# An attention and feed-forward kernel on one core: v moved to partitions 32 to 95, row copies by SyncE, masks on GpSimd, and a new order of the work

## The chip, the cores and the metric

The kernel runs on one core of a Trainium2 chip. The metric is the device time of one execution in microseconds (us), lower is better. Times before the change come from three runs; one further execution was taken with the hardware profiler, and its span (first to last instruction) and its own time stand in the table below.

The engines, by the names that the profile uses: TensorE (PE, its weight loads PEld), VectorE (DVE), ScalarE (ACT), GpSimd (POOL) and SyncE (SP). GpSimd and SyncE also issue transfers, which 16 DMA engines carry out.

## The reference

Four batches, eight heads, 768 positions, 64 elements to a head, all given in float32. Two stages: an attention with a narrow band and one summary key for each block of 32 positions, and a feed-forward layer whose rows are the heads of one position side by side.

```python
block, window = 32, 16
k_sum = k.reshape(B, H, 24, 32, D).max(axis=3)
v_sum = v.reshape(B, H, 24, 32, D).mean(axis=3)
scores_l = where(|i - j| < 16, scale * q @ k.T, -1e9)      # the band
scores_s = scale * q @ k_sum.T + log(32)                   # 24 summary keys
a = softmax(concat(scores_l, scores_s))
attn = a @ concat(v, v_sum)                                # 768 x 64 for each head
x = attn, heads side by side                               # 3072 x 512
h = x @ w_in                                               # 512 -> 2048
out = (h * clip(h + 3, 0, 6) / 6) @ w_out                  # 2048 -> 512
```

## The kernel before, in words

**Tiles.** A query tile has 64 positions. A band of half-width 16 around it touches at most 96 keys, so each query tile multiplies with 96 band keys and 24 summary keys, 120 rows in all. Keys stand in `kaug` (12 tiles of 96 + 24 columns for each pair of heads), queries in `qaug` (`qT` is its view without the first 32 columns), probabilities in `at`, values in `vaug`, of which there are two: batch b uses `vaug[b % 2]`. In `vaug` the partition is the key of the tile: rows 0 to 63 are the 64 positions of the tile, rows 64 to 95 the first 32 positions of the next tile (the "halo"), rows 96 to 119 the 24 block sums. Since the window reaches 64t to 64t + 95, the queries of tile t are positions 64t + 16 to 64t + 79: q is shifted by 16. A row of `vaug` holds 66 elements (132 bytes): 64 of v, and ones (or 32 for the summary rows) that make the softmax's denominator.

**Attention of one batch.** The scores matmul gives 120 x 768 for a pair of heads and half the positions (L519); ScalarE takes the exponential (L527); VectorE multiplies with the 0/1 band mask (L531; batch 0's first half has the mask added in the matmul instead); the values matmul (L632) is 120 deep; VectorE divides by the denominator (L663, L667); TensorE transposes the result (L682) into `x`, feature by position. The block sums of v are a matmul with a 0/1 matrix (`ind`, L552 and L567), copied out and spread over the 12 tiles: by VectorE and ScalarE in batches 0 and 1, by SyncE's transfers (L575) in batches 2 and 3.

**How k and q come in.** Batch 0 is loaded in rows and transposed by TensorE (L448, L493), q in two halves. Batches 1 to 3 are loaded "raw": 32 rows by 96 chunks of 32 elements, four loads for k (L367) and eight for q (L375, two of 16 rows for each group because of the shift), and VectorE transposes 32 x 32 blocks (L588, L592). There is one raw buffer each for k and q, so a batch's loads wait for the transposes of the batch before. v comes in four loads a batch (L385), the halo of batches 1 to 3 in one more load from memory (L393) and a small SyncE copy (L395); batch 0's halo is copied by VectorE or ScalarE.

**The feed-forward layer.** A tile s is half a batch (384 positions). F steps: for each of 16 blocks of 128 hidden features four matmuls of 384 columns into a bank `h` (L700), a relu on ScalarE (L705), a product on VectorE (L707). G steps: for each of three groups of 128 positions 16 matmuls of 512 columns, in quarters of four (L720), then a copy out (L432, a helper's line) and a store by SyncE (L730, L732). The two weight matrices are loaded in four pieces each (L417, L423).

**What sets the order of the work.** Every step is recorded with its engine, a cost, what it reads and writes and the buffers that it takes. `ORDER` is a list of all steps written out in the program. `Plan.run` goes through it, gives each step its buffer and its estimated begin, and the instructions are recorded in that order. Each engine works through its own instructions strictly in order, so what stands behind a waiting instruction waits with it; this holds for GpSimd's and SyncE's issues too. A name in the list reads so: `K21.0` is load 1 of k of batch 2, `Q`, `V`, `H` likewise for q, v and halo, `I` and `O` are the pieces of w_in and w_out, `k`, `q`, `s`, `u`, `h`, `v` are key, query, scores, block-sum, halo and values steps, `w21` the raw transposes of batch 2 and pair 1, `F` and `G` the feed-forward steps; `:A`, `:D` (and in the new list `:P`) say that a step that may run on several engines runs on ScalarE, VectorE or GpSimd. In the first 22 us, matmuls on a constant tile fill TensorE's gaps (L803).

Of the kernel before, what the change touches and what calls it, by code (L numbers as in the profile page):

```python
# [9 lines left out]
F32 = mybir.dt.float32  # L10
# [5 lines left out]
D = 64  # L16
# [5 lines left out]
VW = 66  # L22
# [7 lines left out]
c.0 K00.0 c.7 K01.0 c.10 c.11 c.12 c.13 c.9 c.1 Q000.0 K02.0 Q010.0 c.2 c.3 k00.0 k01.0 q010.0 k01.1 k01.4 k00.1 q010.1:A  # L30
k00.4 c.4 k00.3:A k01.2 s010.0 q030.0 q000.0 q000.1:A s030.0 s010.1 s010.2 q020.0 q020.1:A k00.2 q030.1:D k01.3:D k03.0
k03.1 k02.0 k02.1 V00.0 V01.0 c.6 V02.0 V03.0 I0.0 I1.0 Q001.0 s000.0 u00.0 s000.1 u01.0 k03.3:A k03.2 k02.2 u00.1:D u00.2:D
k03.4 u01.1:D s000.2 u01.2:A u00.3:D k02.4 h21.0:D k02.3:D u02.0 s020.0 s030.1 s020.1 s020.2 u03.0 h30.0:D h00.0:D h10.0:D
h01.0:D v00.0 v02.0 u03.1:D u03.2:D v00.2 u01.3:D v00.3 u02.1:A s030.2 h20.0:A u02.2:A Q011.0 I2.0 I3.0 O0.0 O1.0 O2.0 O3.0
K10.0 K11.0 K13.0 K12.0 v01.0 v01.2 v02.1 v00.1 v02.4 v00.4 v00.5 v02.2 v02.3 v02.5 v00.6 v01.1 v01.3 v01.4 v01.5 h31.0:A
v00.7:A u03.3:A q001.0 q011.0 q001.1:A q021.0 q021.1:A u02.3:D q011.1:D v01.6 v02.6 q031.0 s021.0 v01.7:A h11.0:D v02.7:D
c.5 c.8 s021.1 F00.0 F00.1 F00.2 F00.10 F00.3 F01.0 F01.1 s001.0 s001.1 s021.2 q031.1:D F00.4 F01.2 s001.2 F00.11 F00.12
s011.0 F00.13 F00.14 Q121.0 Q101.0 Q110.0 Q100.0 Q120.0 Q131.0 Q130.0 Q111.0 s011.1 s011.2 s031.0 F00.5 F00.6 F00.7 F01.9
F00.8 F00.9 F02.6 s031.1 F01.3 F02.7 F01.10 F01.4 s031.2 F02.8 v04.0 v03.0 F01.6 F01.11 F01.5 v03.1 v03.2 F01.7 F01.8 v04.1
F02.3 F02.4 F02.5 F02.9 v03.3 v03.4:A F02.10 v04.2 F00.15 F02.0 v05.0 v04.3 F00.16 F02.1 F02.11 F00.17 F02.2 v05.1 v05.2  # L40
F03.3 F03.9 F03.0 v04.4:A F03.4 v05.3 F03.1 F03.10 v05.4:A G01.0 F03.5 F03.11 F03.2 F03.6 F10.0 F03.7 F12.0 F03.8 F10.1
F10.3 F12.1 F10.2 F12.2 F10.6 F10.4 F10.9 F10.5 F10.7 F10.8 F11.0 F10.10 F10.11 F11.6 F11.1 F11.9 F11.2 F11.7 F11.8 F11.10
F11.11 F12.6 F12.7 F12.8 F12.9 F12.10 F12.11 w12.0 G01.1 F13.0 F13.1 w13.0 F13.2 w11.0 w13.3 w10.0 w12.3 G01.2 G01.3 F12.3
F13.9 G01.4:A G02.0 G02.1 G02.2 G02.3 F11.3 F13.10 w11.2:A F12.4 F12.5 G02.4:A w12.2:A F13.3 F11.4 F13.4 w10.2:A w13.2:A
w12.4 w11.3 w11.4 w11.1 w11.5:D G00.0 G00.1 s110.0 s110.1 s110.3 w12.1 w13.1 w12.5:D w13.5:A G00.2 G00.3 s120.0 s120.1
s120.3 w13.4 w10.1 F13.5 w10.3 F11.5 w10.4 w10.5:D F13.11 V10.0 V13.0 V11.0 V23.0 V12.0 H1.0 K20.0 K22.0 V20.0 K21.0 Q231.0
K23.0 Q220.0 V22.0 V21.0 Q200.0 Q221.0 Q201.0 Q211.0 Q210.0 Q230.0 s130.0 G00.4:A F13.6 G12.0 s130.3 s130.1 F13.7 G00.5
G01.5 H1.1 G02.5 s120.2 s110.2 s130.2 s100.0 s100.1 F13.8 s100.2 s110.4 s100.3 G12.1 u1.0 u1.1:A u1.3:A u1.5:A G12.2 G12.3
G12.4:A u1.4:D u1.2:D v10.0 s120.4 v10.1 v10.5 v10.6 v10.2 s100.4 u1.7:A u1.6:A u1.9:A G11.0 G11.1 v12.0 v10.3 v10.4:A
u1.8:A v12.1 v12.2 s130.4 G11.2 v10.7 v12.3 v10.8:D G11.3 v12.4:A v13.0 F20.0 F20.3 G11.4:A F20.1 F20.4 v13.5 v13.1 v13.2  # L50
v13.6 F20.9 v13.3 v15.0 F20.10 F20.2 F20.5 F20.11 v15.1 v15.2 F20.6 F21.0 F20.7 F20.8 F21.1 V30.0 V31.0 V32.0 V33.0 F21.2
w21.0 F21.6 G10.0 F21.7 v13.4:A F21.8 F21.3 v15.3 v13.7 F21.9 F22.3 F21.4 F21.5 w20.0 F22.0 G10.1 F21.10 F22.4 v15.4:A
F21.11 F22.1 F22.5 F22.9 F23.0 F22.2 w20.3 F22.10 F22.11 F23.1 w21.2:A v13.8:A F23.2 w22.0 F22.6 u2.0 F22.7 F22.8 w21.3
G10.2 F30.0 F23.6 G10.3 w22.2:A F30.1 w20.4 F30.2 F30.3 F23.3 G10.4:A w22.3 w22.4 G22.0 G22.1 w20.1 u2.1:A w20.2:A F23.7
F23.4 w20.5:A F30.4 G12.5 u2.3 u2.5 G11.5 u2.4 u2.2 F23.5 F23.8 w22.1 s200.0 s200.1 s200.3 F30.5 w22.5:A F31.6 F23.9 G22.2
w23.1 F23.10 F31.7 s220.0 F23.11 F31.8 w21.4 w21.1 w21.5:D F30.9 G22.3 F31.0 F31.3 s220.3 s220.1 s210.0 G22.4:A H2.0 Q301.0
Q330.0 w23.0 K32.0 Q311.0 H3.0 F31.1 w23.5:A Q310.0 Q300.0 Q320.0 Q331.0 F31.2 F31.4 s200.4 F30.10 F30.11 F31.5 G20.0 G20.1
F30.6 F32.3 F33.0 Q321.0 K33.0 K31.0 K30.0 s210.1 s210.3 w23.3 F30.7 w23.4 s200.2 F30.8 w23.2:A F32.4 F33.1 u3.0 u3.1:D
s220.2 F33.2 s220.4 s210.2 G20.2 s230.0 s230.1 s230.3 s230.2 F32.5 G20.3 F31.9 F32.9 F31.10 F31.11 G20.4:A H2.1 G10.5 u3.3
u3.5 H3.1 G20.5 G22.5 v20.0 v20.1 v20.5 v20.2 v20.6 F33.9 G32.0 F32.10 F33.10 v22.0 F33.3 v20.3 F33.11 F32.0 G32.1 F33.4  # L60
v20.4:A v20.7 F32.1 v20.8:A v22.1 v22.2 F33.5 s230.4 F32.2 s210.4 v22.3 F32.11 v22.4:A F33.6 F32.6 F33.7 F32.7 v23.0 F33.8
v23.1 F32.8 F40.0 F40.1 F41.3 G32.2 F40.9 G32.3 F40.10 F41.4 v23.2 F40.2 F40.11 F41.5 v23.5 v23.6 F42.3 F41.9 F42.4 F42.5
F43.0 v25.0 F41.10 G32.4:A v23.3 F41.11 F42.0 F40.6 G30.0 G30.1 v23.4:A F43.1 F42.1 F40.7 v25.1 w30.1 F42.2 F43.2 F40.8
F41.0 F41.1 F41.2 v25.2 F40.3 F40.4 w30.5:A w33.1 w32.1 F42.6 G30.2 G30.3 F42.9 G30.4:A F42.7 v23.7 v23.8:A F42.10 G21.0
G21.1 G21.2 F40.5 w31.0 F42.8 F42.11 F43.3 F43.4 w30.0 w30.3 F43.6 w30.4 F43.5 w31.3 G21.3 F43.7 w32.5:D G21.4:A G21.5 v25.3
F41.6 G31.0 F43.9 G31.1 G31.2 w31.4 F43.8 v25.4:A F41.7 w30.2:A w33.0 F43.10 w31.2:A F41.8 w31.1 w31.5:D w32.0 F43.11 s300.0
F50.9 G31.3 F50.0 s300.1 s300.3 G31.4:A s310.0 s310.3 F50.1 s310.1 G31.5 u3.2 u3.4 G32.5 G30.5 w33.2:A w32.2:D w33.3 w32.3
w33.5:D F50.2 G40.0 F53.0 F53.1 F50.10 w32.4 w33.4 F50.11 G40.1 G40.2 G40.3 G40.4:A s320.0 s320.1 s320.3 F51.0 F53.3 G42.0
F53.4 s330.0 F51.1 s330.3 s330.1 s310.2 s310.4 F53.2 F53.5 s320.2 s300.2 s330.2 F51.2 G42.1 G42.2 F51.6 F51.7 F51.8 F52.3
v30.0 v30.5 v30.1 v30.6 v30.2 F52.0 F52.1 F52.4 F50.3 v32.0 v32.1 F52.2 F52.5 G42.3 G42.4:A F50.4 v30.3 F52.9 s330.4 G41.0  # L70
F51.3 G41.1 F52.10 v30.4:A v32.2 v32.3 v30.7 F51.4 F50.5 s320.4 F52.11 F51.9 v30.8:A F51.10 F51.5 v32.4:A F50.6 F50.7 F51.11
F50.8 s300.4 F52.6 G41.2 F52.7 F52.8 G41.3 F60.0 F60.1 G41.4:D F60.3 v33.0 F60.4 F60.2 F53.9 F53.10 F53.6 F53.7 F53.8 v33.1
F53.11 F60.5 v33.5 v33.6 G50.0 G50.1 v33.2 G41.5 F62.3 G50.2 F61.9 F61.10 G50.3 F62.4 G50.4:A G42.5 F61.11 v33.3 F62.9 v35.0
G51.0 F60.9 F60.10 v33.4:D F62.5 v35.1 v35.2 v35.3 F62.10 v35.4:A F60.11 v33.7 F60.6 G51.1 G51.2 F60.7 F60.8 F62.11 G51.3
G51.4:D v33.8:A F61.3 F61.0 F61.6 F61.4 F61.1 F61.7 F61.2 F61.5 F61.8 G52.0 F63.3 F70.0 G52.1 F72.6 G52.2 F63.4 F70.1 F70.2
F63.5 F73.0 F63.9 F72.7 F73.1 F63.10 F72.8 F73.2 F63.11 G52.3 G51.5 G50.5 G40.5 F63.0 F62.0 F62.6 F62.1 G52.4:D F62.7 F62.2
G62.0 F62.8 F63.6 F63.1 F63.7 F63.2 G62.1 G62.2 F70.9 F70.6 F63.8 G62.3 F70.10 F70.7 F70.11 G62.4:D F70.3 F71.3 F71.4 F70.8
F71.5 G61.0 G61.1 F72.9 F72.10 F70.4 F72.11 F71.6 F71.7 F70.5 F71.8 G61.2 F73.3 F73.4 F73.5 G61.3 F72.3 F71.0 F71.9 G61.4:D
F71.1 F72.4 F71.2 F72.5 F71.10 F71.11 G60.0 F72.0 F73.6 G60.1 G60.2 G72.0 F73.7 F72.1 F72.2 G62.5 G61.5 G52.5 F73.8 F73.9
F73.10 F73.11 G72.1 G71.0 G71.2 G60.3 G72.2 G71.4 G71.6 G70.0 G60.4:A G71.7:A G71.1 G70.1 G71.8 G60.5 G71.3 G71.5 G71.9  # L80
G70.2 G70.3 G70.4:A G71.10:A G71.11 G70.5 G72.3 G72.4:D G72.5
"""

BANKS = ("S", "h", "o")


SLOW = 8.5
TURN = 0.11
LATER = 19.0
KRAW = 2.0  # L90
LAT = {"PE": 0.16, "ACT": 0.08, "DVE": 0.07}


# [8 lines left out]
class Op:  # L102
    def __init__(self, eng, cost, fn, prio, lat, alloc):
        self.eng, self.cost, self.fn, self.prio, self.lat, self.alloc = eng, cost, fn, prio, lat, alloc
        self.deps, self.bufs, self.end, self.begin, self.dma = set(), [], None, None, 0.0
        self.alloc = [] if alloc is None else alloc if isinstance(alloc, list) else [alloc]


class Plan:
# [11 lines left out]
    def op(self, eng, cost, fn, r=(), w=(), prio=0.0, alloc=None, dma=0.0, lat=None, free=(), touch=(), after=0.0, form="full"):  # L121
# [21 lines left out]
        o.deps.discard(o)  # L143
        self.ops.append(o)
        return o

    def run(self):

        named = {o.key: o for o in self.ops}
# [5 lines left out]
        for token in ORDER.split():  # L155
# [16 lines left out]
            for a in o.alloc:  # L172
                a.begin = t
# [676 lines left out]
```

## Time and profile before

| | us |
|---|---|
| three runs | 233.34, 238.12, 240.46 (median 238.12) |
| the profiled execution | 233.64 |
| its span | 231.9 |
| mean granted TensorE clock, share of full speed | 0.988 |

| engine | busy us | share of the span |
|---|---|---|
| TensorE matmuls | 217.3 | 94% |
| VectorE | 156.7 | 68% |
| ScalarE | 126.5 | 55% |
| GpSimd | 72.8 | 31% |

The busy shares are averages over stages that differ. Matmuls are pipelined, so a busy TensorE is not one at its peak. The strips of the page show the stages: each digit is the busy share of one fortieth of the span (5.8 us) in tenths. The DMA strip counts a slice as busy when the engines have packets under way, whatever these move; the line of GB/s under it shows what they move:

```profile
GB/s 76 169 123 182 191 206 196 119 77 87 95 120 176 186 103 86 85 114 146 84 142 89 127 71 0 45 80 84 3 11 85 0 136 3 0 45 90 3 68 114
```

The high numbers of slices 4 to 7 are the weights, in long rows; the lower ones behind them are the raw loads, in pieces of 64 bytes. A waiting time is shown in square brackets in a timeline, with what ended it; where the engine named had itself been waiting, one looks at that engine next.

### The profile page before, as it was taken

How to read it: one execution, taken by the hardware profiler on the slowest of the kernel's cores; microseconds unless marked ns; L12 is line 12 of the kernel's file. 1: busy time of each engine (PE TensorE's matmuls, PEld its weight loads, DVE VectorE, ACT ScalarE, POOL GpSimd, SP SyncE). 2: the span in 40 equal slices, each digit the busy share in tenths (PEclk: the TensorE clock that was granted, in tenths of full speed). 3: DMA queues.
4: the chain of work that ended last, by engine and by line, in shares of the span. 5: the costliest groups of instructions: out<-in, count | busy, mean ns of one | idle time of the engine just before them, and what ended most of it. 6: DMA issues, size and time to landing. Idle time of an engine off the chain costs nothing.

```text
span 231.9 us, 5321 instructions
## 1 busy us (share of the span) xinstructions
PE 217.3 (94%) x2175; PEld 121.8 (52%) x2175; DVE 156.7 (68%) x327; ACT 126.5 (55%) x258; POOL 72.8 (31%) x86
## 2 busy tenths in 40 slices
PE   7899699999989997989999889999999999999991
PEld 2365476555445563545565445555555555555560
DVE  2489689789897669889785499945955645454201
ACT  2287567774588854768654535675552543434101
POOL 7994481357754734707741200000000000000000
PEclk9999979999999999999999999999999999999998
DMA  5999999999999999999999990132002030012013
GB/s 76 169 123 182 191 206 196 119 77 87 95 120 176 186 103 86 85 114 146 84 142 89 127 71 0 45 80 84 3 11 85 0 136 3 0 45 90 3 68 114
DMA packets 126585, 22.14 MB, mean 95 GB/s; under 512 B 116960, under 2 KB 123616, under 8 KB 126560
## 3 DMA queue, kind: packets, MB, share of 16 engines
q0 software_dynamic: 117280, 14.81, 217.7%
q1 hardware_dynamic: 9280, 6.98, 12.7%
q8 instruction: 17, 0.28, 0.7%
q14 instruction: 8, 0.07, 0.1%
HBM read 29.60 MB, written 6.29 MB: 155 GB/s over the span
## 4 chain that ended last, share of the span: by engine, by line
PE 58%; DMA 18%; issue 9%; POOL 9%; ACT 2%; DVE 2%; DVEq 0%; POOLq 0%
PE h L700 26%; PE o L720 22%; DMA kraw<-in_k_dram 13%; DMA qnat<-in_q_dram 5%; PE h L720 4%; POOL vaug L385 3%; ACT at L527 2%; PE S L519 1%; PE S L632 1%; POOL qraw L375 1%; POOL qnat L357 1%; PE S L682 1%; POOL knat L346 1%; POOL win L417 1%; POOL kraw L367 1%
## 5 line engine op out<-in xcount | busy, mean ns | idle before, releaser
L700 PE MATMUL h<-x,win 128*128 128x384 bf16 (+1 forms) x536 | 95.0, 321 | 3.1 <-DVE g L707 3.1
L705 ACT ACTIVATE r<-h 128x384 f32<-128x384 f32 x128 | 60.4, 493 | 59.4 <-PE h L700 58.7
L707 DVE SCALAR_TENSOR_TENSOR g<-r,h 128x384 bf16<-128x384 f32 x128 | 67.5, 545 | 33.9 <-ACT r L705 32.1
L720 PE MATMUL o<-wout,g 128*128 128x512 bf16 x336 | 82.3, 379 | 0.2 <-ACT ot L432 0.2
L700 PEld LDWEIGHTS <-win 128*128 128x128 bf16 x536 | 49.9, 99 | 37.5 <-issue 3.6
L720 PEld LDWEIGHTS <-g 128*128 128x128 bf16 x400 | 38.1, 98 | 36.3
L375 POOL DMA_DIRECT2D qraw<-in_q_dram x24 | 21.3, 890 | 29.1 <-issue 10.5
L527 ACT ACTIVATE at<-S 120x768 bf16<-120x768 f32 x32 | 24.8, 812 | 7.1 <-PE S L519 7.1
L367 POOL DMA_DIRECT2D kraw<-in_k_dram x12 | 15.8, 1317 | 13.5 <-issue 12.0
L385 POOL DMA_DIRECT2D vaug<-in_v_dram x16 | 15.1, 949 | 4.8 <-PE h L700 3.1
L592 DVE STREAM_TRANSPOSE qaug<-qraw 128x800 bf16<-128x800 bf16 x12 | 11.8, 998 | 6.2 <-DMA kraw<-in_k_dram 3.3
L667 DVE TENSOR_TENSOR xn<-S,rc 128x512 bf16<-128x512 f32 (+1 forms) x25 | 15.7, 643 | 0.4
L531 DVE TENSOR_TENSOR at<-at,mask 96x768 bf16<-96x768 bf16 x28 | 14.8, 546 | 1.5 <-ACT at L527 1.0
L432 ACT COPY ot<-o 128x512 f32<-128x512 f32 x16 | 9.4, 586 | 11.3 <-PE o L720 10.6
L588 DVE STREAM_TRANSPOSE kaug<-kraw 128x768 bf16<-128x768 bf16 x12 | 11.5, 965 | 2.1 <-DMA kraw<-in_k_dram 2.1
L432 ACT COPY x<-S 128x512 bf16<-128x512 bf16 x19 | 11.0, 587 | 2.5 <-PE S L682 2.1
L519 PEld LDWEIGHTS <-kaug 64*128 64x128 bf16 x384 | 7.0, 96 | 8.2 <-issue 6.3
L605 DVE TENSOR_REDUCE red<-kaug 128x24 bf16<-128x768 bf16 x12 | 11.2, 940 | 0.0
L519 PE MATMUL S<-qaug,kaug 64*128 64x64 bf16 x384 | 9.2, 192 | 2.0 <-ACT at L527 1.2
L803 PE MATMUL o<-idle 128*128 128x512 bf16 x30 | 9.5, 442 | 1.5 <-DVE idle L287 1.5
L720 PE MATMUL h<-wout,g 128*128 128x512 bf16 (+1 forms) x64 | 10.9, 326 | 0.0
L632 PEld LDWEIGHTS <-at 120*64 120x64 bf16 x384 | 7.6, 111 | 5.9 <-issue 4.8
(84 smaller groups left out, 139.3 us busy)
## 6 DMA issues: line engine op xcount, KB each, us to landing
out_dram<-ot SPq DMA_DIRECT2D x19, 256.0 KB
vaug<-in_v_dram POOLq DMA_DIRECT2D x16, 192.0 KB, 10.7
kraw<-in_k_dram POOLq DMA_DIRECT2D x12, 192.0 KB, 14.8
qraw<-in_q_dram POOLq DMA_DIRECT2D x24, 96.0 KB, 11.9
win<-in_moe_w_in_dram POOLq DMA_DIRECT2D x4, 512.0 KB, 11.8
wout<-in_moe_w_out_dram POOLq DMA_DIRECT2D x4, 512.0 KB, 13.5
vaug<-in_v_dram POOLq DMA_DIRECT2D x3, 380.0 KB, 16.2
out_dram<-ot SPq DMA_DIRECT2D x4, 224.0 KB
```

What stands on the lines that cost most here:

```text
L367: op("POOL", 0.8, lambda hs=hs, ds=ds, rows=rows: nc.gpsimd.dma_start(out=kraw[rows], in_=k[b, hs].rearrange("h (c r) d -> r (h c) d", r=B ...
L375: nc.gpsimd.dma_start(out=qraw[lo:lo + PAD, 1 - x:1 - x + NP * NB], in_=src[PAD * (1 - x):PAD * (2 - x)])
L385: op("POOL", 0.95, lambda: nc.gpsimd.dma_start(out=o[0:QB, lo:hi, 0:D], in_=rows[:, lo:hi]), w=[("v", b % 2, c)], prio=prio, dma=1.7)
L432: {"ACT": nc.scalar.copy, "DVE": nc.vector.tensor_copy, "POOL": nc.gpsimd.tensor_copy}[eng](o, i)
L519: nc.tensor.matmul(X[p, half].slot[:, j, i * QB:(i + 1) * QB], kaug[p][rows, t], qT[rows, p, t * QB:(t + 1) * QB], start=not masked, stop= ...
L527: op("ACT", act(2 * HALF), lambda a=a, x=x: nc.scalar.activation(a, x.slot[0:KEYS, :, 0:HALF], AF.Exp, scale=scl), r=[x], w=[("at", p, hal ...
L531: op("DVE", dve(2 * HALF, 1.92), lambda m=m, half=half: nc.vector.tensor_tensor(m, m, mask[:, half * HQ:(half + 1) * HQ].unsqueeze(1).to_b ...
L667: nc.vector.tensor_tensor(o, src[..., 0:D], r.unsqueeze(len(r.shape)).to_broadcast(list(o.shape)), op=ALU.mult)
L700: nc.tensor.matmul(h.slot[:, lo * 128:hi * 128], w_in_sb[:, kt, ft * 128:(ft + 1) * 128], xt[s].slot[:, kt, lo * 128:hi * 128], start=(kt ...
L705: op("ACT", act(HALF), lambda: nc.scalar.activation(r.slot[:], h.slot[:, 0:HALF], AF.Relu, bias=0.5, scale=1.0 / 6.0), r=[h], w=[r], prio= ...
L707: op("DVE", dve(HALF), lambda: nc.vector.scalar_tensor_tensor(gt[s].slot[:, ft], r.slot[:], 1.0, h.slot[:, 0:HALF], op0=ALU.min, op1=ALU.m ...
L720: nc.tensor.matmul(o.slot[:, a:z], gt[s].slot[:, ft, ts * 128:(ts + 1) * 128], w_out_sb[:, ft, a:z], start=(ft == 0), stop=(ft == NFT - 1))
```

## The change

- **Where v stands.** The 64 positions of a tile move from partitions 0 to 63 to partitions 32 to 95, and partitions 0 to 31 take the last 32 positions of the tile before. The window of tile t is now 64t - 32 to 64t + 63, its queries 64t - 16 to 64t + 47. A raw load of q needs no shift any more: four loads of 32 rows a batch instead of eight of 16. A row of `vaug` takes 80 elements (160 bytes) instead of 66. The block-sum matmul reads partitions 0 to 95 with zeros in `ind` for the first 32, so those partitions are set to zero once beforehand (five memsets of 32 x 24 x 32 words on VectorE, three on GpSimd).
- **The rows ahead** ("halos"). For batches 2 and 3 they no longer come from memory through GpSimd's queue: SyncE copies them within SBUF, 3040 pieces of 128 bytes, once v has landed. For batch 1 VectorE and ScalarE copy them. The block sums of batches 2 and 3 go through SyncE as before; batch 1's are copied by ScalarE, VectorE or GpSimd.
- **Masks on GpSimd.** The band mask may run on VectorE or GpSimd; in the new order 15 of 28 run on GpSimd, between its issues.
- **Buffers.** k and q raw have two buffers each; the second pair shares its space with batch 0's row buffers and serves batch 2.
- **Batch 0.** q's second half comes in three loads of 128 rows with all heads side by side (`qwide`), transposed 128 x 128. The values of pairs 2 and 3 of the first half are two matmuls each, 96 deep on v and 24 deep on the block sums (`vf`), so these sums are not spread first.
- **The order.** A new `ORDER`. In the plan's estimate a raw load costs 1.6 instead of 2.0, a load of v 1.25 instead of 1.7, SyncE's transfers add to the same line of loads as GpSimd's, and GpSimd may have 7 loads and 14400 elements under way.

The diff, cut to its core:

```diff
-VW = 66
+VW = 80
-KRAW = 2.0
+KRAW = 1.6
     def run(self):
...
             if o.dma and e == "SP":
-                o.end += o.dma + 1.8 + 0.5 * min(max(line - o.end, 0.0), 4.0)
+                o.end, line = o.end + o.dma + 1.8 + min(o.dma, max(line - o.end, 0.0)), max(line, o.end) + o.dma
             elif o.dma:
-                line = max(line, o.end + 1.5) + 1.06 * o.dma
-                o.end = line + 0.9
+                line = max(line, o.end + 1.0) + 1.06 * o.dma
+                o.end = line + 0.8
+                self.queue.append((o.end, o.els))
...
-    kraw = sb([128, NP * NB, BLK], BF16, "kraw")
-    qraw = sb([128, NP * NB + 1, BLK], BF16, "qraw")
+    first = sb([128, 2 * NP * NB, BLK], BF16, "first")
+    kraw, qraw = ([sb([128, NP * NB, BLK], BF16, f"{n}raw"), first[:, i * NP * NB:(i + 1) * NP * NB]] for i, n in enumerate("kq"))
...
     def load_v(b, c, prio):
-        op("POOL", 0.95, lambda: nc.gpsimd.dma_start(out=o[0:QB, lo:hi, 0:D], in_=rows[:, lo:hi]),
-           w=[("v", b % 2, c)], prio=prio, dma=1.7)
+        op("POOL", 0.95, lambda: nc.gpsimd.dma_start(out=o[BLK:WIN, lo:hi, 0:D], in_=rows[:, lo:hi]),
+           w=[("v", b % 2, c)], prio=prio, dma=1.25, els=1536)
...
-    def load_vhalo(b, prio):
+    def halos(b, prio):
...
-        op("POOL", 0.75, lambda: nc.gpsimd.dma_start(out=o[QB:WIN, 0:n - 1, 0:D], in_=rows[0:WIN - QB, 1:n]),
-           w=[("vh", i, c, x) for c in range(NP) for x in range(2)], prio=prio, dma=3.2)
+        op("SP", 0.7, lambda: nc.sync.dma_start(out=o[0:BLK, 1:n, 0:D], in_=o[QB:WIN, 0:n - 1, 0:D]),
+           r=[("v", i, c) for c in range(NP)], w=every, free=[("vz", i, c) for c in range(NP)], prio=prio, dma=3.4)
...
     def scores(b, parts, prio):
...
-            op("DVE", dve(2 * HALF, 1.92), lambda m=m, half=half: nc.vector.tensor_tensor(
+            op(("DVE", "POOL"), {"DVE": 0.62, "POOL": 1.75}, lambda eng, m=m, half=half: ENGINE[eng].tensor_tensor(
```

The part of the new list around the loads of batch 2, as it stands (each engine takes its own names from it in this order; K, Q and V are GpSimd's issues, as are the steps marked `:P`):

```
V10.0 Q11.0 Q12.0 Q13.0 Q10.0 ...
G00.4:A s110.1 w10.5:A s110.3 G12.0 F13.3 s100.0 F13.4 w12.5:A s100.1 s100.3 V20.0 V22.0 V21.0 V23.0 K21.0 u1.2:P K20.0 K22.0 s110.2:P
s100.2:P K23.0 u1.3:P s100.4:P ...
v10.5 v10.6 v10.1 v10.2 Q22.0 s120.4:P s130.4:P Q23.0 Q20.0 Q21.0 G12.4:A ...
F20.8 F20.11 w20.1 w21.1 F21.0 F21.1 F20.3 G11.3 F20.4 w20.5:A F20.5 G11.4:A F22.3 F22.4 F21.2 w22.3 F22.5 s200.0
```

## The prediction

> **What bounds the kernel now.** I read the page's strips first, then TensorE's waits, then VectorE's waits at the same places, then the DMA issues one at a time.
>
> ```profile
> PE   7899699999989997989999889999999999999991
> PEclk9999979999999999999999999999999999999998
> DMA  5999999999999999999999990132002030012013
> ```
>
> Each digit is 5.8 us. TensorE looks full throughout, but the DMA engines are never without work until slice 24 (about 139 us) and nearly idle after. So two things can bound: TensorE's work, and the arrival of loads up to 139 us. Where TensorE waits between 80 and 140 us shows which:
>
> ```profile
> 88.57 1.46 PE L700 MATMUL h<-x,win 128*128 128x384 bf16 x8 [1.37 <-DVE g L707]
> 100.57 0.53 PE L519 MATMUL S<-qaug,kaug 64*128 64x64 bf16 x24 [0.79 <-DVE qaug L592]
> 134.14 2.11 PE L700 MATMUL h<-x,win 128*128 128x384 bf16 x12 [1.73 <-DVE g L707]
> ```
>
> The engine named is VectorE, but it had itself been waiting for a load:
>
> ```profile
> 87.10 0.98 DVE L588 STREAM_TRANSPOSE kaug<-kraw 128x768 bf16<-128x768 bf16 x1 [2.05 <-DMA kraw<-in_k_dram]
> 99.51 1.01 DVE L592 STREAM_TRANSPOSE qaug<-qraw 128x800 bf16<-128x800 bf16 x1 [1.82 <-DMA qraw<-in_q_dram]
> 132.64 1.01 DVE L592 STREAM_TRANSPOSE qaug<-qraw 128x800 bf16<-128x800 bf16 x1 [3.30 <-DMA kraw<-in_k_dram]
> ```
>
> So batch 2's q lands at 99.4, its first transpose starts at 99.51 and its first scores at 100.57. Landing times come from the DMA issues in narrow windows (issue start plus us to landing); the first row below was issued at 28.65, the second at 32.78, the third at 52.19, then the halo rows at 59.36 and 96.33, and the last K pair at 126.44 and 127.7:
>
> ```profile
> kraw<-in_k_dram POOLq DMA_DIRECT2D x1, 192.0 KB, 16.0
> kraw<-in_k_dram POOLq DMA_DIRECT2D x1, 192.0 KB, 19.1
> qraw<-in_q_dram POOLq DMA_DIRECT2D x1, 96.0 KB, 9.7
> vaug<-in_v_dram POOLq DMA_DIRECT2D x1, 380.0 KB, 13.5
> vaug<-in_v_dram POOLq DMA_DIRECT2D x1, 380.0 KB, 16.5
> kraw<-in_k_dram POOLq DMA_DIRECT2D x1, 192.0 KB, 10.4
> kraw<-in_k_dram POOLq DMA_DIRECT2D x2, 192.0 KB, 10.5
> ```
>
> K of batch 1 lands from 44.7 to 51.9: 2.4 us for each 192 KB. Its q ends at 61.9: 2.5 us for each 192 KB. The five V behind it end at 69.8 (1.6 us each), the first halo at 72.9 (3.1 us); the second halo, beside SyncE's sums, takes 5.5 (107.3 to 112.8). Only the last two K, with nothing behind them, land 1.4 us apart.
>
> As a sum: first hidden-layer matmul at 30.3; from the chain of waits a group of four costs 0.65 us (L700) or 0.86 us (L720). Counting instructions in the built order, 63.1 us of TensorE work lie between 30.3 and batch 2's first scores and 122.5 us behind them. Each change of matmul form adds about 0.11 us (an L700 pair is 1.30 alone, 1.41 behind scores). Then 99.4 + 1.2 (transpose to scores) + 122.5 + 2.3 (some 21 form changes) + 1.7 (the wait at 134) + 4.6 (tail from 227.3) = 231.7, against a span of 231.9. The profiled execution took 233.64 (1.74 outside the span); the runs shown go from 233.34 to 240.46 with median 238.12, so it is one of the quick ones.
>
> **The change part by part.**
>
> *The start.* q's second half no longer holds the first hidden-layer matmul back (it waits 1.62 us at 27.2 and then works off 3 us of q and scores). I put that matmul at 27.7 instead of 30.3; the three 128-row q loads sit behind 192 KB of K and the first w_in piece, which sets that time. Five zero memsets (768 words each, near 0.75 us by the 0.48 us row for 512) go mostly into VectorE's 4.5 us of idleness before 6.85. Worth -2.6 us if nothing later waits, 0 if batch 2 waits; I take 0, since it does.
>
> *The load stream up to batch 2's q.* Batch 1's halo load goes: -3.1. V rows land at a step of 160 bytes instead of 132: between 1.6 us (no help) and 1.1 us (the K price of an element, 2.4 us for 3072, times 1536), I take 1.4, near the known row, on 12 loads: -2.4 (0 to -6). q comes in 4 loads of 32 rows instead of 8 of 16: K's shape, so K's price; over both batches -1.6 (0 to -8, if 1.4 us held). K itself keeps its shape: 0 (0 to -8 likewise). The plan's own cost for such a load falls from 2.0 to 1.6, and no row in a full stream supports that. New in the stream: SyncE's row copy for batch 2 (3040 elements) and the sums (2304), which the built order places right behind V of batch 2, so while K and q of batch 2 are on their way. In the kernel before the sums went out at 97.6 to 107; the loads then landing (four V and the second halo, 99.4 to 112.8) took 3.2 us longer than their rows above, after 0.65 us for a store. With 3.1 for the copy that is 6.3; part of it fills gaps, so I take 4.7 (0 to 10). Together: 99.4 - 3.1 - 2.4 - 1.6 + 4.7 = 97.0.
>
> By the Trainium skill ("DMA: Bandwidth & Descriptors", "Why small descriptors are slow (HBM only)") a copy inside SBUF does not pay the small-element penalty: its 436 GB/s make an estimate of 0.9 us for the 389 KB copy, and with it the sum is some 2 us lower. The same page ("Issuing engines are not separate DMA queues") says that SyncE's and GpSimd's transfers interleave on the same 16 engines, which speaks against this change, and the late halo (5.5 us against 3.1) agrees.
>
> *GpSimd's queue.* 15 of 28 masks leave VectorE (0.546 us each, -8.2 us of VectorE, hidden beside TensorE's work). No row has such a mask on GpSimd: at least 0.55 (VectorE's), at most 2.3 (its affine_select does 384 elements in 0.58, so twice the elements and twice the inputs); I take 1.75, nearer its own row. What is queued behind them: the last three q loads of batch 2. Batch 1's q now comes behind its V and lands at about 66 (61.9 + 5.6 for V, -1.6 for faster V and q); scores 1.4 later, their exps 0.8 each. GpSimd then runs, in order, one K issue (1.3), two masks, a K issue, a copy (about 1), a mask, a q issue, two masks, and only then three q issues: 68.9 + 8.75 + 1.3 + 1 + 1.3 + 3.9 = 85.2 at its end; the quickest landing behind other loads is 9.1 to 10.4 us from issue, so 93 to 95. It sits just under 97.0: no extra term, but a small delay shows.
>
> By the Trainium skill ("GPSIMD Engine Reference", "Elementwise — side-by-side cycle accounting") a two-input op costs 2.6 cycles an element, an estimate of 1.7 us for 768; no run here shows it yet.
>
> *The order.* This decides. In the new order batch 2's first scores stand behind 56.3 us of TensorE work (40 hidden tiles, 25 output quarters) instead of 63.1 (49 and 26): 130.0 us lie behind them instead of 122.5. If TensorE waits there for q, it does 7.5 us less while waiting. When would it not wait? 27.7 + 56.3 + 0.5 (slow-clock stretch) + 2.6 (form changes) = 87.1, so q would have to land by 85.7.
>
> *Elsewhere.* K and q of batch 3 go to a second pair of buffers and need not wait for the transposes of batch 2 (the 8.3 us GpSimd wait at 97.7 goes): the 1.7 us at 134 goes. The last output half is 256 columns on ScalarE with one store instead of 512 on VectorE (0.69) with two issues: -0.8, tail 3.8. Behind the late q VectorE has four transposes (4.0), two reductions (1.9), a K transpose and twelve 0.545 us products against 12 us of matmuls: +1.0.
>
> *Sum.* 97.0 + 1.4 + 130.0 + 2.4 + 1.0 + 3.8 = 235.6 span, 237.3 with the 1.74 outside: +1.6% against 233.64. Three runs do not say whether the profiled run (233.64) or the median (238.12) is typical; I add half of their 4.5, so 239.5, against 235.9 for the kernel before in the same terms.
>
> **The rivals.** Spans are turned into times by +1.74 and +2.2.
>
> *B, GpSimd's head of line (slower).* Masks at 2.3 us, or exps late behind ScalarE's relus, push the last q issue to 88 to 90 and its landing to 100 to 104. It decides from q at 98 on: span 238.6 to 242.6, time 242.5 to 246.5. For: five masks and a copy stand ahead of those loads. Against: the loads are queued deep.
>
> *C, loads at the price of the last K pair (faster).* 1.4 to 1.7 us for 192 KB and a cheap SyncE copy: batch 1's q at 61, GpSimd's last q issue near 80, landing 87 to 92: span 225.6 to 230.6, time 229.5 to 234.5. For: the 1.4 us row. Against: 2.4 and 2.5 in the full stream.
>
> *D, nothing waits.* The start's gain and VectorE's relief come through: 27.7 + 186.3 + 0.5 + 5 (form changes) + 3.8 + 1 = 224.3, time 228.
>
> That the change doesn't do what it says is no case: its masks, copies and loads all stand in the built order.
>
> **How the numbers follow.** The forecast (A, q at 93 to 98.5, time 235.5 to 241) 0.41; B 0.29; C 0.22; D 0.08. 2% is about what a measurement of this kernel can tell from no change: bounds 231.2 and 240.6. Faster: D and 0.12 of C, 0.20. Slower: B and 0.09 of A, 0.38. Same: 0.42. The range 229.5 to 247 leaves out D and the ends of B; A alone is 235.5 to 241.
>
> **What would show it.** Right: TensorE idle in front of batch 1's and batch 2's first scores, VectorE ahead of it waiting for loads into the second raw buffer, these landing near 97, and no wait near 134. Wrong: raw loads under 1.8 us apart in a full stream, GpSimd masks well off 1.75, or batch 2's first scores before 92 us.

## The result, and the profile after

The changed kernel takes 234.73 us (median of 20 runs, 233.62 to 237.12); the kernel before, beside it, 233.73 (20 runs, 231.64 to 240.46). The ratio is 1.010, 95% interval 1.006 to 1.014. Some executions of a kernel are slower as a whole; here and below the medians are of all executions, the ratios and their intervals of the fast ones alone. The forecast was 239.5, by a wait for batch 2's q. That wait did not come; other losses came, and they ate what the change gained. The profiled execution took 233.88, its span is 232.2 (before: 233.64 and 231.9).

The strips of the changed kernel's page:

```profile
PE   5998999999895799999989999999999999999993
PEclk9999999999997589999999999999999999999999
DMA  5999999999999999059996111252100011011123
```

Against the strips before, two things are new. TensorE has a dent in slices 12 and 13 (70 to 81 us), and its granted clock falls to 5 tenths in slice 13. The loads are done sooner: the DMA engines run empty for the first time in slice 16 (93 us), not in slice 24. TensorE's waits of half a microsecond and more from 30 us on, as its timeline shows them (start, us, engine, line, operation, and in brackets the idle time ahead and what ended it):

```profile
62.65 0.59 PE L559 MATMUL S<-qT,kaug 64*128 64x64 bf16 x24 [0.90 <-DVE qT L629]
73.49 1.89 PE L764 MATMUL o<-wout,g 128*128 128x512 bf16 x4 [2.65 <-DVE g L751]
77.20 0.92 PE L673 MATMUL S<-vaug,at 120*64 120x65 bf16 x26 [1.52 <-DVE at L572]
121.24 0.81 PE L744 MATMUL h<-x,win 128*128 128x384 bf16 x4 [0.73 <-DVE g L751]
```

None stands in front of batch 2's scores. The waits at 88, 100 and 134 us of the kernel before are gone, and 4.2 us of waiting at 71 to 77 us are new, in batch 1's masks and values. Both name VectorE. What it did then (its timeline):

```profile
66.00 0.97 DVE L629 STREAM_TRANSPOSE qT<-qraw 128x768 bf16<-128x768 bf16 x1
66.89 0.51 DVE L751 SCALAR_TENSOR_TENSOR g<-r,h 128x384 bf16<-128x384 f32 x1
67.33 1.18 DVE L572 TENSOR_TENSOR at<-at,mask 96x768 bf16<-96x768 bf16 x1
70.69 1.70 DVE L465 COPY vaug<-vs 24x768 bf16<-24x768 bf16 x1
73.35 3.80 DVE L572 TENSOR_TENSOR at<-at,mask 96x768 bf16<-96x768 bf16 x1
```

and GpSimd, in the same stretch:

```profile
66.46 1.64 POOL L572 TENSOR_TENSOR at<-at,mask 96x768 bf16<-96x768 bf16 x1 [0.70 <-ACT at L568]
70.34 1.82 POOL L572 TENSOR_TENSOR at<-at,mask 96x768 bf16<-96x768 bf16 x1
73.50 3.23 POOL L572 TENSOR_TENSOR at<-at,mask 96x768 bf16<-96x768 bf16 x2
```

Lay the two side by side. VectorE's mask that began at 73.35, 0.15 us ahead of GpSimd's pair, ended 0.42 us behind that pair: 3.80 us for an operation of 0.55. The copy of 0.35 us took 1.70 beside GpSimd's mask of 70.34. VectorE's transpose (0.97) and product (0.51), which ran beside GpSimd's mask of 66.46, kept their durations. GpSimd's masks nearly did: 13 of the 15 took 1.63 to 1.65, and the two that began while a VectorE mask was under way (70.34 and 163.77 us) took 1.82 and 1.95. Over the whole kernel, GpSimd's masks cost what the prediction took (1.75), and VectorE's cost twice what they did before (0.546), by the groups of instructions (busy, mean ns; the last line is from the kernel before):

```profile
L572 POOL TENSOR_TENSOR at<-at,mask 96x768 bf16<-96x768 bf16 x15 | 24.9, 1673 | 55.3 <-ACT at L568 54.3 <-ACT qT L465 0.9
L572 DVE TENSOR_TENSOR at<-at,mask 96x768 bf16<-96x768 bf16 x13 | 13.5, 1053 | 0.8 <-ACT at L568 0.5
L531 DVE TENSOR_TENSOR at<-at,mask 96x768 bf16<-96x768 bf16 x28 | 14.8, 546 | 1.5 <-ACT at L527 1.0
```

The Trainium skill ("SBUF — State Buffer", section "Who interferes with whom") says that VectorE's second read interface is shared with GpSimd: an operation with two SBUF inputs, or a copy in a two-port mode, is fully blocked while GpSimd reads there, and one with a single input outside those modes is not. The rows agree with it on every kind: masks and copies held (3.80, 1.70), transposes and products with PSUM not. The same page of the Trainium skill also gives the ports to whichever issues first. Two records of other runs agree: a VectorE copy that began 0.03 us ahead of a GpSimd mask (69.59 us, the changed kernel again) and a VectorE mask that began 0.09 us ahead of one (69.56 us, two masks moved) took their usual 0.36 and 0.54. The mask of 73.35 also began first, but GpSimd was then still in the issue of a load (72.12 to 73.48), and it was held; why is open.

The table of stretches shows what followed (columns: engines' busy time, then TensorE's granted clock, the DMA share and GB/s):

```profile
70.00:75.00 5.00, 2.35 (x8) 0.63 (x6) 4.96 (x6) 1.66 (x3) 4.91 (x4) 0.77 1.83 134
75.00:80.00 5.00, 3.48 (x41) 1.58 (x42) 4.90 (x7) 1.41 (x2) 5.00 (x5) 0.50 2.15 134
80.00:85.00 5.00, 5.00 (x50) 2.58 (x52) 3.52 (x6) 1.24 (x3) 4.24 (x4) 0.71 2.87 150
```

In narrower stretches the clock is 0.50 from 72.7 to 82.9 us: it fell while TensorE was waiting. Busy time times the missing clock gives 2.35 x 0.23 + 3.48 x 0.50 + 5.00 x 0.29 = 3.7 us.

So the gain and the loss: the first hidden-layer matmul starts at 26.6 instead of 30.3 (-3.7); TensorE's idle time behind it rises from 5.3 to 6.0 (+0.7), since 4.2 us of new waits stand against the waits that went; the slow clock, which before cost about 1 us behind that matmul (0.53 from 30 to 32 us), now costs 3.7 (+2.7); TensorE has 0.7 us more work by instructions (+0.7); the tail is 3.5 instead of 4.6 (-1.1). That adds up to -0.7 against +0.3 of span; 1 us is not accounted for.

### The profile page after: what moved, and what is told of

It is laid out like the page before. It is cut to its first block, busy times and chain, and to the rows that moved or that the text cites. A ratio compares the mean times of both kernels' runs of the same rounds, so it can differ in the third digit from the quotient of the medians.

```text
span 232.2 us, 5327 instructions
## 1 busy us (share of the span) xinstructions
PE 218.8 (94%) x2168; PEld 121.5 (52%) x2168; DVE 163.5 (70%) x313; ACT 129.0 (56%) x274; POOL 91.0 (39%) x91
## 4 chain that ended last, share of the span: by engine, by line
PE 74%; DVE 10%; DMA 8%; POOL 4%; ACT 2%; issue 1%; DVEq 0%; POOLq 0%
PE h L744 28%; PE o L764 25%; PE h L764 4%; DMA qraw<-in_q_dram 4%; DMA kraw<-in_k_dram 4%; PE o L850 3%; PE S L673 3%; DVE at L572 3%; DVE g L751 2%; POOL at L572 2%; PE S L726 2%; PE S L559 2%; DVE vaug L465 2%; DVE qT L629 2%; ACT at L568 1%
## 5 line engine op out<-in xcount | busy, mean ns | idle before, releaser
L764 PE MATMUL o<-wout,g 128*128 128x512 bf16 x336 | 85.5, 389 | 2.8 <-DVE g L751 2.6
L744 PEld LDWEIGHTS <-win 128*128 128x128 bf16 x536 | 49.4, 98 | 36.4 <-issue 1.8
L572 POOL TENSOR_TENSOR at<-at,mask 96x768 bf16<-96x768 bf16 x15 | 24.9, 1673 | 55.3 <-ACT at L568 54.3
L568 ACT ACTIVATE at<-S 120x768 bf16<-120x768 f32 x32 | 25.4, 813 | 0.8 <-PE S L559 0.7
L416 POOL DMA_DIRECT2D vaug<-in_v_dram x16 | 15.2, 952 | 5.6 <-DMA win<-in_moe_w_in_dram 2.9
L572 DVE TENSOR_TENSOR at<-at,mask 96x768 bf16<-96x768 bf16 x13 | 13.5, 1053 | 0.8 <-ACT at L568 0.5
L405 POOL DMA_DIRECT2D qraw<-in_q_dram x8 | 10.5, 1310 | 6.8 <-issue 5.7
L405 POOL DMA_DIRECT2D kraw<-in_k_dram x8 | 10.6, 1326 | 3.0 <-DMA win<-in_moe_w_in_dram 1.6
L673 PE MATMUL S<-vaug,at 120*64 120x65 bf16 x352 | 9.2, 204 | 1.5 <-DVE at L572 1.5
L559 PE MATMUL S<-qT,kaug 64*128 64x64 bf16 x384 | 9.0, 191 | 1.0 <-DVE qT L629 0.9
```

What stands on the lines that cost most here:

```text
L405: op("POOL", 1.32, lambda src=src, o=o, hs=hs, ds=ds, rows=rows: nc.gpsimd.dma_start(out=o[rows], in_=src[b, hs].rearrange("h (c r) d -> r ...
L559: nc.tensor.matmul(X[p, half].slot[:, j, i * QB:(i + 1) * QB], kaug[p][rows, t], qT[rows, p, t * QB:(t + 1) * QB], start=not masked, stop= ...
L568: op("ACT", act(2 * HALF), lambda a=a, x=x: nc.scalar.activation(a, x.slot[0:KEYS, :, 0:HALF], AF.Exp, scale=scl), r=[x], w=[("at", p, hal ...
L572: op(("DVE", "POOL"), {"DVE": 0.62, "POOL": 1.75}, lambda eng, m=m, half=half: ENGINE[eng].tensor_tensor(m, m, mask[:, low(half):low(half) ...
L673: nc.tensor.matmul(y, a[:, cols], vaug[b % 2][0:KEYS, h, t, 0:D + 1], start=True, stop=True)
L744: nc.tensor.matmul(h.slot[:, lo * 128:hi * 128], w_in_sb[:, kt, ft * 128:(ft + 1) * 128], xt[s].slot[:, kt, lo * 128:hi * 128], start=(kt ...
```

## The experiments

The theory (M, with K for its second half): the masks on GpSimd hold VectorE, VectorE makes TensorE wait, and the wait brings half clock. The rivals: VectorE is simply too full (V); loads or SyncE's transfers hold TensorE (L); the clock falls for another reason (P). All times, each beside runs of the kernel before on the same chip (where the changed kernel did not run on that chip, ratios are compared):

| kernel | median us | before, same chip | ratio, 95% interval | span of its profile |
|---|---|---|---|---|
| all 15 masks on VectorE | 232.10 | 236.05 | 0.983 (0.976 to 0.989) | 230.7 |
| batch 1's five on VectorE | 229.92 | 236.05 | 0.972 (0.964 to 0.980) | 228.9 |
| two of them on VectorE | 231.49 | 236.05 | 0.979 (0.971 to 0.986) | 230.1 |
| 17 filler matmuls, masks as changed | 233.27 | 236.05 | 0.986 (0.980 to 0.993) | 230.2 |
| changed kernel again | 235.11 | 234.22 | 1.006 (0.998 to 1.014) | 233.8 |
| changed, v's row 132 bytes | 235.73 | 234.22 | 1.011 (1.006 to 1.015) | 237.4 |
| before, v's row 160 bytes | 233.43 | 234.22 | 0.984 (0.970 to 0.998) | 230.3 |
| batch 1's on VectorE, 5 fillers | 229.67 | 234.22 | 0.977 (0.967 to 0.987) | 227.8 |
| the same without SyncE's row copy | 229.77, one run | 234.57 | - | 228.1 |
| batch 1's on VectorE, again | 231.47 | 234.57 | 0.987 (0.977 to 0.998) | 227.9 |
| with 5 fillers, again | 230.72 | 234.57 | 0.986 (0.979 to 0.993) | 228.0 |
| all on VectorE, 5 fillers | 229.68 | 234.57 | 0.982 (0.975 to 0.990) | 229.1 |

### All GpSimd masks back on VectorE

```diff
-s110.2:P s100.2:P s100.4:P s120.4:P s130.4:P s200.2:P ... s310.4:P
+s110.2:D s100.2:D s100.4:D s120.4:D s130.4:D s200.2:D ... s310.4:D
```

> All 15 masks that the changed kernel runs on GpSimd run on VectorE again, at the same places of the list; nothing else is different. Theory M (in the changed kernel VectorE's operations on SBUF are held while GpSimd runs a mask; that held VectorE back by some 6 us between 59 and 77 us, made TensorE wait 2.65 + 1.52 us and then cost about 3.7 us of slow clock): VectorE's masks take 0.55 us again, each; the wait at 73 shrinks to under 1.5 us, the clock stays above 0.9 there; the 15 masks add 8.2 us of VectorE, mostly hidden: 227 to 230 us. Rival V (VectorE needed the relief; its backlog, not the masks' company, made the wait): the five masks more of batch 1 make the waits longer, 235 to 239. Rival L (loads or SyncE's transfers hold TensorE): unchanged, 234 to 236.

VectorE's 28 masks take 0.568 us on average again, and the wait at 73 is 1.46. Rivals V and L fall: more work on VectorE made the kernel faster. The time is above the forecast of M. The profile shows a part of it: in this execution batch 1's q landed later, TensorE waited 2.97 us for it at 62.5 us, and the clock was 0.62 between 66 and 70 us.

### Only batch 1's masks, and only two of them

```diff
-s110.2:P s100.2:P s100.4:P s120.4:P s130.4:P
+s110.2:D s100.2:D s100.4:D s120.4:D s130.4:D
```

> Only the five GpSimd masks of batch 1 go to VectorE; the ten of batches 2 and 3 stay on GpSimd. Theory M: the wait at 73 and the slow clock behind it go, 227 to 230 us, and VectorE's masks of batches 2 and 3 keep what GpSimd costs them there; if those cost nothing, this is equal to or a little faster than all 15 on VectorE. Rival V: 235 to 238. Rival L: 234 to 236.

> Only the two GpSimd masks that ran beside VectorE's mask of 3.80 us (pairs 2 and 3, second half, batch 1) go to VectorE, which then has 1.1 us more to do there. Theory M: VectorE's mask takes 0.55 instead of 3.80, so TensorE's second wait (1.52) is under 0.5; the first (2.65, which comes from the operations before) stays at about 2.6, so the gap is about 2.9 us in place of 4.2, and the slow clock is less or gone: 229 to 233. Rival V: no gain, 234 to 236.

With all five on VectorE its waits of this stretch are these:

```profile
63.80 0.59 PE L559 MATMUL S<-qT,kaug 64*128 64x64 bf16 x24 [1.80 <-DVE qT L629]
71.33 0.81 PE L744 MATMUL h<-x,win 128*128 128x384 bf16 x4 [1.04 <-DVE g L751]
```

M holds: the 4.2 us of waits at 71 to 77 became 1.04. (The copy of 32x640, two instructions, took 0.42 us, against 1.06 in the changed kernel. There no mask ran beside it but GpSimd's issues of q loads, 76.67 to 79.33: VectorE's copies that began during an issue are often held to its end, while masks beside issues alone kept 0.55.) With only the pair of 73.5 us on VectorE, the mask of 3.80 took 1.25 (another GpSimd mask ran beside it until 75.61; it ended 0.42 us behind that one too), and the only wait from 66 to 90 us is

```profile
78.04 0.44 PE L673 MATMUL S<-vaug,at 120*64 120x65 bf16 x16 [0.39 <-DVE xn L711]
```

I had expected the wait of 2.65 to stay; it went too. In this execution batch 1's q came later and GpSimd's other masks met other operations, so this profile does not say that the two masks alone made that wait. Both kernels still had half clock once, behind a wait for batch 1's q (1.80 and 2.19 us).

Masks that leave GpSimd also let it issue its loads earlier, which is a rival to M: with all five on VectorE the last q of batch 2 landed at 82.3 us instead of 89.1. But with only two moved it landed at 91.6, later than in the changed kernel, and that kernel was faster too (0.979). The loads do not explain the gain.

### Filler matmuls in the waits

```diff
+        if o.eng == "PE" and o.key in {"G12.3": 11, "v10.0": 6}:
+            todo.append(lambda n=FILLERS[o.key], s=idle_[-1]: keep(n, s))
         todo.append(o.fn)
```

> The changed kernel with 17 matmuls more on the constant tile (128 x 512 each, 0.216 us): 11 ahead of the output quarter that waits at 73.5 us and 6 ahead of the values that wait at 77.2; their result is not used. TensorE is then busy while it waits. Theory K (the slow clock of 0.50 to 0.77 between 73 and 82 us follows from TensorE's idleness there): the clock stays above 0.9, and about 3 of the 3.7 us come back: 231 to 232.5 us. Rival P (the clock falls there for another reason, such as the work done before): the clock falls all the same, 234.5 to 236.

VectorE's masks are as slow as in the changed kernel (mean 1074 ns), but TensorE has something to do:

```profile
73.28 1.04 PE L764 MATMUL o<-wout,g 128*128 128x512 bf16 x4 [0.27 <-DVE g L751]
77.00 0.60 PE L673 MATMUL S<-vaug,at 120*64 120x65 bf16 x26 [1.18 <-DVE at L572]
...
75.00:80.00 5.00, 3.47 (x59) 1.85 (x58) 4.87 (x9) 0.79 (x1) 5.00 (x4) 1.00 1.94 135
```

(the last line is from the table of stretches). The clock is 1.00 where it was 0.50. K holds, P falls. The mean clock of every execution says the same: 0.976 to 0.985 in the 20 of the changed kernel, 0.997 to 1.000 in the four with fillers. Work that nobody needs brought the ratio from 1.010 (1.006 to 1.014) to 0.986 (0.980 to 0.993), with the masks where the change put them. The half clock was then the greater part of the loss (in this execution batch 1's q also came in time).

### The changed kernel again

> The changed kernel itself, as the yardstick on this chip for the runs beside it: 1.006 to 1.014 times the kernel before. Theory K (a wait of TensorE of about 1.8 us or more is followed by half clock for 3 us or longer, one of up to 1.73 us is not) says of its profile: every stretch of half clock stands behind such a wait, whichever wait it is in this execution.

In this execution batch 1's q came later, the masks met other operations, and the same thing happened elsewhere. VectorE, GpSimd and TensorE, from the three timelines:

```profile
75.77 4.40 DVE L465 COPY vaug<-vaug 32x640 bf16<-32x640 bf16 x2
```

```profile
76.66 3.23 POOL L572 TENSOR_TENSOR at<-at,mask 96x768 bf16<-96x768 bf16 x2
```

```profile
64.35 0.59 PE L559 MATMUL S<-qT,kaug 64*128 64x64 bf16 x24 [2.25 <-DVE qT L629]
81.07 0.44 PE L673 MATMUL S<-vaug,at 120*64 120x65 bf16 x16 [3.70 <-DVE xn L711]
```

Now it is the copy of 32x640 that is held, 4.40 us instead of 0.42: 0.9 us beside GpSimd's issue of a q load (75.28 to 76.64), then beside the same pair of masks. TensorE waits 3.70 us for what comes behind it. The clock is half behind both waits (0.50 at 66 to 68, 0.52 at 82 to 84 us), as K said. Which operation is caught is chance; in all four profiles with the masks where the change put them, one is.

### v's row of 132 or 160 bytes, alone

```diff
-VW = 80
+VW = 66
```

(in the changed kernel; in the kernel before the other way round)

> The changed kernel with v's row of 66 elements (132 bytes) as before; all else as changed. Theory R (v's row step of 160 bytes made its loads quicker): the four v loads of batch 2 land about 1.6 us apart instead of 1.25, K and q behind them keep 1.5 to 2.0, q of batch 2 lands about 1.5 us later, hidden; time within 1% of the changed kernel. Rival S (the row step is not it; the loads are quicker because the queue holds other loads): v lands 1.25 us apart all the same. Rival W (the row step matters to all loads beside v): K and q are 2.4 apart and q of batch 2 lands at 95 or later, time up by 2 us or more.

> The kernel before with v's row of 80 elements (160 bytes), nothing else. Theory R: v's loads land 1.2 to 1.3 us apart instead of 1.6, the halo loads take less than 3.1 and 5.5, K and q stay at 2.4 and 2.5; q of batch 2 lands 4 to 5 us earlier (12 loads are ahead of it in all, of which those behind K of batch 1 count), so 231 to 233 where the kernel before takes 235. Rival S: no difference at all. Rival W: K and q also fall below 2.0, and q of batch 2 lands at 90 or earlier.

Theory R holds for v: in the kernel before, the five loads of v behind batch 1's q landed 1.6 us apart (61.9 to 69.9) with 132 bytes and 1.3 apart (63.4 to 69.8) with 160. In the changed kernel the four v loads of batch 2 took 1.5 each with 132 bytes (66.0 to 71.9) and 1.3 with 160 (61.6 to 66.8). It reaches no other load, so rival W falls. In the kernel before, q of batch 2 was to land 4 to 5 us earlier and landed at 99.6 instead of 99.4: GpSimd's last q issues waited for earlier loads to finish (3.0 and 1.5 us), and the microsecond or two was lost there. The ratio is 0.984, from executions that go from 230.77 to 239.07; its profile lacks the waits at 88 and 134 us, but that the row step removed them is not shown. The run with 132 bytes was profiled in an execution of 239.16 us, well above its median; only its load spacing is used here.

### What SyncE's row copy costs the loads

```diff
-        op("SP", 0.7, lambda: nc.sync.dma_start(out=o[0:BLK, 1:n, 0:D], in_=o[QB:WIN, 0:n - 1, 0:D]),
+        op("SP", 0.7, lambda: b == 2 or nc.sync.dma_start(out=o[0:BLK, 1:n, 0:D], in_=o[QB:WIN, 0:n - 1, 0:D]),
```

(and the second, small transfer likewise), in the kernel with batch 1's masks on VectorE and 5 fillers

> The kernel with batch 1's five masks on VectorE, and 5 matmuls on the constant tile (1.1 us in all, result not used) ahead of batch 1's first scores, where TensorE waited 1.80 us for q and then had a clock of 0.5 for 3 us. Theory K: the wait is at most about 1 us, no half clock behind it: 1 to 1.5 us gained where q is late, up to 1 us lost where it is in time; 228.5 to 230 on a chip where the kernel without them takes 229.9. Rival P (the clock falls there anyway): 230.5 to 231.5.

> The kernel with batch 1's masks on VectorE and 5 filler matmuls, with SyncE's copy of the rows ahead of batch 2 left out (both of its transfers; the values of batch 2 then use rows that are batch 0's). It prices SyncE's transfers in the stream of loads. With the copy (issued at 75.8 us) two loads of q and one of K landed 4.5, 3.8 and 4.1 us after the load before them, where 1.8 is usual. Theory T (the row copy takes its turn on the same DMA engines and costs the loads beside it some 4 us, about as the prediction's 4.7 for copy and sums said): q of batch 2 lands by 84.5 instead of 87.3 and q of batch 3's last load by 91 instead of 94.8; the time does not change, as TensorE does not wait for these (229 to 230.5). Rival U (the sums' eight transfers or the issue times do it, the copy costs nothing): q of batch 2 still lands at 87 or later.

The last q load of batch 2, issued at 73.17 with the copy and at 74.17 without it (DMA issues in narrow windows, us from issue to landing in the last column):

```profile
first<-in_q_dram POOLq DMA_DIRECT2D x1, 192.0 KB, 14.1
```

```profile
first<-in_q_dram POOLq DMA_DIRECT2D x1, 192.0 KB, 8.2
```

It lands at 87.3 with the copy, at 82.4 without. This one load is a poor measure, though: in other profiles with batch 1's masks on VectorE and the copy in place it lands at 82.3, 84.9 and 88.7, by which of the loads the copy meets. The end of the train is steadier: the last q of batch 3 issued in it lands at 94.0 to 96.4 in those four profiles and at 89.9 without the copy; counted from batch 2's last k, 18.8 to 20.2 us against 14.2. So the copy costs the stream about 5 us, in the time of loads that are under way, and theory T holds for the stream. The Trainium skill's 436 GB/s for a copy inside SBUF ("DMA: Bandwidth & Descriptors", "Where 436 GB/s comes from") gave an estimate of 0.9 us; these 3040 pieces of 128 bytes cost five times that, so the measurement decides against that estimate. It did not show in the time (one execution of 229.77, beside 229.74 to 231.28 for the same kernel with the copy on that chip), since TensorE does not wait for these loads.

### What the fillers and the last ten masks are worth

> Batch 1's five masks on VectorE, nothing else, once more, beside the two that follow. Theory K: its profile has a wait for q of batch 1 ahead of the first scores (64 us), of 0 to 3 us from execution to execution, and half clock behind it where it is 1.8 or more; median 0.97 to 0.98 of the kernel before.

> The same with 5 filler matmuls ahead of batch 1's first scores. Theory K: no half clock, 0 to 1 us quicker in the median than without them, and closer together from run to run. Rival: their 1.1 us of work costs what the clock gives, no difference.

> All 15 masks on VectorE, with the same 5 fillers, so that half clock behind the wait for batch 1's q does not blur the comparison. It tells what the ten masks of batches 2 and 3 are worth on GpSimd. Theory N (nothing: VectorE has room for 5.5 us more there, and its own masks are no longer held): equal to the kernel beside it within 0.5 us. Rival G (they are worth something: with all masks on VectorE the run without fillers took 232.1 us where that with ten of them on GpSimd took 229.9): 1.5 to 2.5 us slower than the kernel beside it.

With the fillers no stretch from 24 to 140 us has a clock under 0.95 in either profile with batch 1's masks moved. Without them TensorE waited 1.87 us for q, and this time the clock stayed at 1.00; a wait of 1.80 had halved it in the first run. The traces show why. In all 14 the granted clock changes only on a grid of 3.41 us: every stretch at one clock between two changes is a whole multiple of it. On that grid the wait of 1.80 lay in one step and left TensorE 1.47 us of work in it; the wait of 1.87 was cut by a border at 62.85 and left 1.77 in the fuller step (TensorE's busy time, clock, DMA):

```profile
61.49:64.90 3.41, 1.47 (x29) 1.00 2.82 144
64.90:68.31 3.41, 3.41 (x32) 0.50 4.30 134
```

```profile
62.85:66.26 3.41, 1.77 (x30) 1.00 3.19 140
66.26:69.67 3.41, 3.03 (x60) 1.00 5.95 122
```

This holds in every trace here while TensorE still has work ahead: the ten steps at full clock with 1.52 us of work or less were each followed by half clock, no step with 1.69 or more was. Once at half clock, steps with 1.62 to 2.28 us of work were followed by another one at half clock and steps with 3.08 or more by full clock, which is why 2.65 + 1.52 us of waits in the changed kernel cost three steps.

The medians, 231.47 and 230.72, can't be told apart. With all masks on VectorE the time is 229.68: rival G falls. It is 1.0 us below the kernel beside it, more than the 0.5 that N allowed, but the two intervals overlap, so the ten masks of batches 2 and 3 show no gain on GpSimd. The 2.2 us between the first two kernels of the table stay unexplained: both profiles have half clock once, for 3.41 us, and TensorE's waits in the first are longer (2.97 and 1.46 us against 1.80 and 1.04). Every kernel with batch 1's masks on VectorE is below the kernel before and below the changed kernel (0.972 to 0.987 against 1.006 and 1.010).

## Why the prediction was right or wrong

**The failed step is "The load stream up to batch 2's q".** It said 97.0; the last q of batch 2, issued at 79.31, landed at 89.1, and its transposes began at 92.8 with no wait for a load (no brackets in VectorE's timeline):

```profile
first<-in_q_dram POOLq DMA_DIRECT2D x1, 192.0 KB, 9.8
```

```profile
92.81 1.83 DVE L629 STREAM_TRANSPOSE qT<-first 128x768 bf16<-128x768 bf16 x2
```

Piece by piece: batch 1's q was to land at about 66 and landed at 61.6. From there v and k of batch 2 were to take 4 x 1.4 + 4 x 2.4 = 15.2 us and took 11.7 (to 73.3): v 1.3 each, k 1.6. The 15.8 that this left up to 97.0 for batch 2's q and SyncE's transfers were right (15.8, part of it GpSimd running masks instead of issuing). So the error is the price of k and q: I stayed at 2.4 and 2.5, from k right behind the weights and from q in half loads of 16 rows, and whole loads in a train land 1.5 to 2.1 us apart. That is the prediction's own first sign of being wrong, raw loads under 1.8 us apart in a full stream. The 2.4 was a mean over unlike rows: batch 1's k in the kernel before landed 1.9, 1.9, 2.9 and 2.4 us behind the load before it. And the row of the last K pair, which I kept as the lower end and for rival C, was misread: 10.5 is the middle of two loads that took 10.4 and 10.7, so the second landed 1.6 us behind the first and not 1.4. That 1.6 is what k of batch 2 then took. What makes k quicker than in the kernel before is not separated: v's row step is excluded, q's pieces and the order are not.

**"Batch 2 would wait, so the start is worth 0"** fell with it. The earlier start came through (26.6 instead of 27.7 forecast and 30.3 before) and was spent at 71 to 83 us instead. That the time still came out inside the stated range is luck: the wait that was forecast did not come, and waits and half clock that the prediction did not have came in its place. The 2.2 us added because the profiled execution might be a quick one were not there either: the 20 runs of the kernel before have a median of 233.73, beside 233.64 for that execution.

**GpSimd's queue.** The mask's price was right (1.67 against 1.75). Its cost was looked for in the wrong place: I asked what is queued behind it and held VectorE's relief for hidden, and did not ask what VectorE can do meanwhile. The relief of VectorE was costed at a gain that is hidden, never at a loss; this is the second step that failed, a term put at nothing. In fact the ten masks of later batches show no gain, and the five of batch 1 hold VectorE for longer than they free it (5 x 0.55 = 2.7 us of work less, against 3.25 + 1.35 + 0.63 us more in three held operations alone).

**SyncE's transfers.** Right in kind and size: the copy alone costs some 5 us of the stream, where 4.7 was taken for copy and sums. It fell on loads that nobody waited for.

**The order.** q was to land by 85.7 if TensorE was not to wait. It landed at 89.1 and was not waited for, since TensorE was by then late itself, by 4.2 us of waits and 3.7 of half clock; with batch 1's masks on VectorE and fillers it landed at 87.3, and 2.5 us of other waits and 1.1 of fillers were enough. Of the rivals, C comes nearest on the loads, and D, "nothing waits, 228", is what the kernels with batch 1's masks on VectorE come near: 229.67 to 232.10. None of the four had the mechanism that decided. The wait near 134 went, as said, though one of 0.73 at 121 took its place. The tail was 3.5 (3.8 said).

## What to carry to other kernels

Moving an elementwise step to GpSimd is not only a matter of its own duration and queue: look at which VectorE operations will run beside it, and count those with two SBUF inputs and copies within SBUF as held for as long as GpSimd runs. And price a wait of TensorE at more than its length: where it takes about 1.9 us out of one 3.41-us step of the clock's grid, the next step runs at half clock and costs up to 1.7 us more. So where a wait can't be removed, matmuls on a constant tile in it may pay. For loads, take the spacing inside an undisturbed train of the same shape, not one beside others.

## What the runs showed of the hardware

- VectorE's mask took 3.80 us and its copies 1.70 and 4.40 us instead of 0.55, 0.35 and 0.42 while GpSimd ran masks; part of the 4.40 lies beside GpSimd's issue of a load. Transposes (0.97) and products with a PSUM operand (0.51) kept their durations; GpSimd's masks took 1.63 to 1.65, and 1.82 and 1.95 where they began during a VectorE mask.
- VectorE's copies can be held by GpSimd's issues of loads too: one of 24x768 that began 0.55 us into an issue took 0.92 us instead of 0.35 and ended 0.16 us behind it (69.92 us, first run with 5 fillers), and the copy of 32x640 took 1.06 instead of 0.42 in the changed kernel. Not every copy beside an issue was held, and masks beside issues alone were not.
- Half clock came and went on a grid of 3.41 us. It followed each step at full clock in which TensorE had at most 1.52 us of work, and none with 1.69 or more (14 traces, while TensorE had work ahead); it lasted one step (3.41 us), or two or three where the next steps had 1.62 to 2.28 us of work. By the length of a wait alone there is no sharp limit: single waits of 1.80, 2.19 and more were followed by it, those of 1.53, 1.73 and 1.87 were not, and in the kernel before 1.62 and 0.40 us close together were (28.5 to 31.9 us). The Trainium skill ("TensorE: Matmul & The Clock Gate", "What's actually happening") speaks of an activity window of about 3.4 us that runs free, with half rate after an idle one. The grid agrees with the window; but no step here had to be wholly idle, 1.9 us of idleness in it were enough.
- A load of v (192 KB) landed 1.3 us behind the one before where its rows in SBUF step by 160 bytes and 1.5 to 1.6 us where they step by 132, each in one profile of two kernels.
- A copy of 3040 pieces of 128 bytes within SBUF delayed the train of loads beside it by about 5 us (its end at 94.0 to 96.4 us with the copy, 89.9 without).
